# Attention probabilities split into float16 parts and transposed by DMA, V products in float16, second layer in plain float32

## The chip, the cores and the metric

The kernel runs on one core of one Trainium2 chip. The metric is device time in microseconds (us) of one execution. Before the change it is 1511.71 us, the median of 3 runs (1510.98 to 1515.28).

## The reference

Attention keeps only the keys whose score lies within tau of the row's maximum. Its output goes through two layers with a rational function between them.

```python
# q, k, v: (8, 8, 576, 64) float32; tau = 0.02
def _attn_ref(q, k, v, tau):
    scale = 1.0 / np.sqrt(q.shape[-1])
    scores = scale * np.matmul(q, k.transpose(0, 1, 3, 2))
    thresh = np.max(scores, axis=-1, keepdims=True) - tau
    scores = np.where(scores >= thresh, scores, -1000000000.0)
    scores = scores - np.max(scores, axis=-1, keepdims=True)
    attn = np.exp(scores)
    attn = attn / (np.sum(attn, axis=-1, keepdims=True) + 1e-09)
    return np.matmul(attn, v).astype(np.float32)

# x: (4608, 512), the heads side by side; w_in: (512, 2048), w_out: (2048, 512), random doubles
def _moe_ref(x, w_in, w_out, a, b):
    h = x @ w_in
    h2 = h * h
    h3 = h2 * h
    P = a[0] + a[1] * h + a[2] * h2 + a[3] * h3
    Q = 1.0 + np.abs(b[0]) * np.abs(h) + np.abs(b[1]) * h2
    g = P / (Q + 1e-06)
    return (g @ w_out).astype(np.float32)
```

## The kernel before

**Tiles.** There are 8 batches of 4 head pairs. A pair has five units: four full ones of 128 queries of both heads, and a remainder unit that holds the last 64 queries of both heads. That makes 160 units, 128 full and 32 remainders. In the code a unit is named by its pair (0 to 31) and its number in it, so `e13_1` is the probability tile of pair 13, unit 1.

**A unit.** PE multiplies queries and keys in float32 into PSUM (L617, L628). DVE takes the row maximum (L638). Then the mask: in three units of five ACT computes the exponential (L649) and DVE multiplies it with the mask and sums the row (L663); in the other two ACT does both with two activations (L655, L659), a steep leaky ramp and an exponential with a row sum. `BY_ACT` says which. DVE makes the reciprocal of the sum. PE transposes the probabilities in blocks of 128 x 128 float32 (L689, L698 or L701), and with them a tile that repeats the reciprocals (L702). ACT copies the transposed blocks out of PSUM (L263, L706). PE multiplies V with them, with V's 64 columns as weights, one head in each half of the array (L718). DVE multiplies the result by the transposed reciprocals (L723) and two operations split it into a float16 part and a remainder, `xh` and `xl`.

**The layers.** A step takes 256 tokens through two blocks of 128 of the 2048 hidden columns. There are 144 steps. The first layer has 24 float16 matmuls of 256 columns a step (L829), three products of parts of x and w_in. Then ACT and DVE compute the rational function, with a logarithm and an exponential for 1/Q. Its value is split into a rounded part and a remainder (`gh`, `gl`), and the second layer adds three products in the rounded float32 form per block and half of the tokens, 12 matmuls of 512 columns a step (L892).

**The weights** come as doubles. ACT and DVE take them apart once, at the start.

**Order.** Nothing is in a hand-written order. Every operation is entered with its engine, or a choice of engines with a cost for each (`FLEX`), a due time and the buffers and PSUM banks that it takes and gives back. `Plan.order` then goes through them and writes one order for each engine, which the chip keeps: each engine does its instructions in that order and waits where data is not there yet. DMA issues are operations of SP's queue. `POOLS` is the number of buffers of each kind, `PRICE` how a costly engine weighs against a cheap one, `TPD` (new) the cost that the planner puts on a transpose. Until the planner's time 400, it fills part of PE's planned idle time with matmuls whose result is not used (`f_warm`).

The scores of the first 25 units use one bank pair for each head; later units use the one set of three banks (`B3`) for both heads, so the scores of a unit wait until that set is free.

Of the kernel before, what the change touches and what calls it, by code (L numbers as in the profile page):

```python
# [23 lines left out]
POOLS = {"e": 3, "pT": 2, "st": 4, "sc": 2, "t": 9, "g": 2, "x": 4, "xr": 1, "wo": 16}  # L24

B2, B3, BA, B1 = [(0, 1), (2, 3), (4, 5)], [(0, 1, 2)], [(3,), (4,), (5,), (6,), (7,)], [(7,), (6,), (5,), (4,), (3,)]
# [13 lines left out]
BY_ACT = (5, (1, 3))  # L40
# [3 lines left out]
FLEX = {"f1": {"ACT": 0.66, "DVE": 0.345}, "f6": {"DVE": 0.62}, "s1": {"ACT": 0.65, "DVE": 0.396},  # L44
        "d1": {"ACT": 0.55, "DVE": 0.345}, "d2": {"DVE": 0.62}, "qs": {"ACT": 0.7, "DVE": 0.42},
        "s2": {"DVE": 0.66},
        "vmax": {"ACT": 0.58, "DVE": 0.68}, "thr": {"DVE": 0.155}, "rb": {"DVE": 0.16, "ACT": 0.22},
        "tpo": {"ACT": 0.5}, "xh": {"ACT": 0.211, "DVE": 0.15}, "xl": {"DVE": 0.212}, "r": {"ACT": 0.74, "DVE": 0.345},
        "r2": {"DVE": 0.613}, "gl": {"DVE": 0.613}, "gh": {"ACT": 0.541, "DVE": 0.345}}
# [3 lines left out]
PRICE = {"ACT": 1.0, "DVE": 5.0}  # L53

TOL = {"PE": 0.08, "ACT": 0.129, "DVE": 0.1, "POOL": 0.1, "DMA": 0.0}
# [23 lines left out]
class Plan:  # L79
# [3 lines left out]
    LAT = {"PE": 0.27, "ACT": 0.28, "DVE": 0.22, "POOL": 0.16, "DMA": 2}  # L83
    OWN = {"PE": 0.0, "ACT": 0.15, "DVE": 0.13, "POOL": 0.1, "DMA": 2.0}
# [136 lines left out]
def masked_attention_rational_ffn(  # L221
# [159 lines left out]
    def decode_ops(i, key, load, hold, stay):  # L381
# [26 lines left out]
        def f6():  # L408
            t = box["w"].bitcast(I32)
            if stay:  # L410
                tensor_tensor(box["rw"][:, :, 1], t, box["rw"][:, :, 0], ALU.add)
                box["w"] = box["rw"][:, :, 1].bitcast(F32)
            else:
                tensor_tensor(t, t, box["rw"][:, :, 0], ALU.add)

        l = op("DMA", 1.5, key - 2.0, ld, (), [hold])
# [4 lines left out]
        o6 = op(FLEX["f6"], 0, key, f6, [o5, o2], (), [ht if stay else hold])  # L421
        return o6, box, ht
# [7 lines left out]
    for i in range(NW):  # L430
        pieces = []
        for c in range(NC):
# [3 lines left out]
            def load(n=n, c=c, i=i):  # L436
                rw = wpool.tile([P, 2, WS], F32, name=f"rwi{n}", tag="wo", bufs=NF).rearrange("p a b -> p (a b)")
                rw = words(rw)
                nc.sync.dma_start(rw, win_[c * P:(c + 1) * P, 2 * i * WS:2 * (i + 1) * WS].rearrange("p (n two) -> p n two", two=2))
                return rw  # L440
            key = w_key(i, c)

            o6, box, _ = decode_ops(n, key, load, hold, True)
# [25 lines left out]
    for f in range(NF):  # L469
        hold = Hold("wo", 1)  # L470

        def load(f=f):
            rw = words(wpool.tile([P, 2, WS], F32, name=f"rwo{f}", tag="wo", bufs=NF).rearrange("p a b -> p (a b)"))
            nc.sync.dma_start(rw, wout_[f * P:(f + 1) * P, :].rearrange("p (n two) -> p n two", two=2))
            return rw
        key = w_key(f // NC, NC + f % NC)
        o6, box, ht = decode_ops(NC * NW + f, key, load, hold, False)
        ht.uses = 2
        hw = Hold("wo", -1)

        def d1(f=f, box=box):
            wo[f] = wpool.tile([P, 2, WS], F32, name=f"wo{f}", tag="wo", bufs=NF)
            copy(fr(wo[f][:, 0]), box["w"])

        def d2(f=f, box=box):
            tensor_tensor(fr(wo[f][:, 1]), box["w"], wo[f][:, 0], ALU.subtract)
        o9 = op(FLEX["d1"], 0, key, d1, [o6], [hw], [ht])
        wo_done.append(op(FLEX["d2"], 0, key, d2, [o9], (), [ht]))

# [12 lines left out]
    Vs = [const.tile([P, NT * P + 2 * D], F32, name=f"V{i}") for i in range(NV)]  # L502
# [7 lines left out]
    def load_ops(bp):  # L510
# [6 lines left out]

        def ldq():
            nc.sync.dma_start(QQ[0:D, 0:S], qT[bb, pr, :, 0:S])
            nc.sync.dma_start(QQ[D:P, 0:NT * P], qT[bb, pr, :, S + REM:])  # L520
            nc.sync.dma_start(QQ[D:P, S:], qT[bb, pr, :, S:S + REM])

        def ldk():
            nc.sync.dma_start(KK[0:D, REM:], kT[bb, pr, :, 0:S])
            nc.sync.dma_start(KK[D:P, 0:S], kT[bb, pr, :, S:2 * S])

        lq = op("DMA", 0.9, p - (4.6 if first else 4.0), ldq, before)
        lk = op("DMA", 0.9, p - (4.5 if first else 3.9), ldk, before)
# [3 lines left out]
    def load_v_ops(bp):  # L532
# [4 lines left out]
        def ld():  # L537
            nc.sync.dma_start(
                t[:, 0:NT * P].rearrange("p (c d) -> p c d", c=NT),
                v[bb, 0:NT * P, pr * P:(pr + 1) * P].rearrange("(c p) d -> p c d", p=P))  # L540
            for hh in range(2):
                nc.sync.dma_start(
# [13 lines left out]
        l = op("DMA", 1.0, max(q, -2.0 + 0.1 * pr), ld, [av_done.get(bp - NV)])  # L556
        v_done[bp] = l
        hv = [Hold("t", 1)]
        vm_ops.setdefault(bb, []).append(op(FLEX["vmax"], 0, max(q + 1.0, p - 1.0), mx, [l], hv, hv))
        if pr == NP - 1:  # L560
            isx_done[bb] = scale_ops(p, lambda: vms[bb], 14, isx[:, bb:bb + 1], None, vm_ops[bb], f"x{bb}")
# [17 lines left out]
    def unit_ops(bp, t):  # L579
# [6 lines left out]
        QQ, KK, V = QQs[bp % NQ], KKs[bp % NQ], Vs[bp % NV]  # L586
# [3 lines left out]
        e_hold = Hold("e", 2 * nh + 3)  # L590
        st_hold = Hold("st", 1)
        w = P if full else REM
        nb = 2 * NT if full else NT
# [72 lines left out]
        def f_rec():  # L666
            r = box["st"][:, 6:6 + nh]
            engines[plan.eng].tensor_scalar(r, box["st"][:, 4:4 + nh], 1e-9, isx[:, bb:bb + 1], ALU.add, ALU.mult)
# [5 lines left out]
        def f_rb():  # L674
            r = box["st"][:, 6:6 + nh]
            rb = bass.AP(r.tensor, r.offset, [list(r.ap[0]), [1, nh], [0, P // nh]])
# [385 lines left out]
```

## Time and profile before

| | |
|---|---|
| median of 3 runs | 1511.71 us |
| profiled execution | 1513.04 us, its span 1511.1 us |
| granted PE clock, mean | 0.987 |
| PE busy | 1452.7 us, 96% of the span |
| ACT busy | 1267.0 us, 84% |
| DVE busy | 1236.3 us, 82% |
| DMA | 56.39 MB, mean 37 GB/s |

A group's row in the profile gives line, engine, operation, output and inputs, sizes, the count, then busy us and mean ns of one, then idle time of the engine just before and what ended it. Where an engine's instructions overlap, the sum of the groups is above the engine's busy time. A plain float32 matmul of the code appears as two instructions in the trace. Attention is over near 1345 us; what follows are steps of the layers alone.

### The profile page before, as it was taken

Reading aid. Unit: us, or ns where it says so; the run is one execution under the profiler, and the core shown is the slowest. Engines: PE = TensorE matmul, PEld = TensorE weight load, DVE = VectorE, ACT = ScalarE, POOL = GpSimd, SP = SyncE. Lnnn points to the kernel's source line nnn. Section 1 sums busy time; section 2 is a strip of 40 time slices with the busy share of each in tenths; the row PEclk is TensorE's granted clock in tenths of the full one; section 3 lists DMA queues with packets and bytes.
Section 4 is the critical chain, followed back from the end, with each engine's and each line's share of the span. In section 5 each row is a group of like instructions: output and inputs, shape, how many; then the busy total and the mean of one; then the engine's idle time right before and its main releaser. Section 6 shows DMA issues by size and latency. Waiting matters only on the chain.

```text
span 1511.1 us, 29010 instructions
## 1 busy us (share of the span) xinstructions
PE 1452.7 (96%) x11230; PEld 1112.4 (74%) x11230; DVE 1236.3 (82%) x2794; ACT 1267.0 (84%) x2560; POOL 2.3 (0%) x17
## 2 busy tenths in 40 slices
PE   7999896999999999999999999999999999999996
PEld 5676674777777777777777777777777777778774
DVE  7988978979788787869697878787969878877778
ACT  7898987989788898979797979897978798877776
POOL 0000000000000000000000000000000000000000
PEclk9999998999999999999999999999999999999998
DMA  5512301011010100010100010101010010000000
GB/s 155 187 38 88 115 25 58 23 38 39 25 38 25 38 25 31 25 36 12 39 17 31 17 38 25 36 19 39 16 32 25 17 31 17 15 1 15 15 15 14
DMA packets 45241, 56.39 MB, mean 37 GB/s; under 512 B 11824, under 2 KB 28208, under 8 KB 45104
## 3 DMA queue, kind: packets, MB, share of 16 engines
q1 hardware_dynamic: 45104, 54.55, 11.8%
q8 instruction: 88, 1.44, 0.4%
q14 instruction: 49, 0.40, 0.1%
HBM read 45.09 MB, written 9.44 MB: 36 GB/s over the span
## 4 chain that ended last, share of the span: by engine, by line
PE 82%; DVE 7%; ACT 6%; DMA 3%; issue 1%; SPq 1%; ACTq 0%; DVEq 0%
PE banks L892 25%; PE banks L829 21%; PE banks L617 11%; PE banks L718 11%; PE banks L689 8%; PE banks L628 4%; DMA rwo<-in_w_out_dram 1%; PE banks L702 1%; DMA QQ<-in_qT_dram 1%; PE banks L698 1%; DVE st L638 1%; DMA rwi<-in_w_in_dram 1%; DVE e L663 1%; ACT pT L263 1%; ACT vj L553 1%
## 5 line engine op out<-in xcount | busy, mean ns | idle before, releaser
L892 PE MATMUL banks<-wo,gm 128*128 128x512 f32 x1536 | 419.5, 411 | 20.2 <-ACT hsm L838 15.7
L829 PE MATMUL banks<-xh,wi 128*128 128x256 f16 x2048 | 376.1, 273 | 2.9 <-ACT pT L263 2.9
L829 PEld LDWEIGHTS <-wi 128*128 128x128 f16 x3456 | 329.5, 98 | 63.3 <-issue 27.6
L892 PEld LDWEIGHTS banks<-wo,gm 128*128 128x128 f32 x1536 | 274.0, 191 | 80.0 <-ACT hsm L838 17.1
L638 DVE TENSOR_REDUCE st<-banks 128x1 f32<-128x576 f32 x288 | 215.0, 753 | 89.3 <-PE banks L628 53.9
L829 PE MATMUL banks<-xl,wi 128*128 128x256 f16 x1024 | 279.5, 273 | 0.0
L617 PE MATMUL banks<-KK,QQ 64*128 64x512 f32 (+3 forms) x784 | 214.8, 538 | 4.1 <-ACT QQ L271 2.1
L263 ACT COPY pT<-banks 128x512 f32<-128x512 f32 x288 | 164.9, 585 | 51.6 <-PE banks L689 49.9
L718 PE MATMUL banks<-pT,V 128*64 128x128 f32 (+1 forms) x3200 | 195.8, 269 | 5.3 <-ACT pT L706 5.3
L718 PEld LDWEIGHTS banks<-pT,V 128*64 128x64 f32 x3200 | 160.2, 138 | 44.9 <-issue 18.6
L689 PE MATMUL banks<-ident,e 128*128 128x128 f32 x1152 | 166.9, 276 | 9.3 <-DVE e L663 4.8
L689 PEld LDWEIGHTS banks<-ident,e 128*128 128x128 f32 x1152 | 133.4, 145 | 25.0 <-ACT pT L263 4.2
L663 DVE SCALAR_TENSOR_TENSOR e<-banks,st,e 128x576 f32<-128x576 f32 x160 | 126.8, 814 | 19.9 <-ACT e L649 19.4
L617 PEld LDWEIGHTS banks<-KK,QQ 64*128 64x128 f32 (+1 forms) x784 | 88.1, 188 | 66.2 <-issue 47.7
L649 ACT ACTIVATE e<-banks,st 128x576 f32<-128x576 f32 x160 | 118.9, 746 | 1.9 <-DVE st L638 1.9
L628 PEld LDWEIGHTS banks<-KK,QQ 128*128 128x128 f32 x432 | 56.3, 190 | 81.9 <-issue 81.9
L859 DVE SCALAR_TENSOR_TENSOR qm<-qm,cf,Am 128x512 f32<-128x512 f32 x128 | 95.5, 746 | 25.6 <-ACT qm L846 25.3
L655 ACT ACTIVATE e<-banks,st 128x576 f32<-128x576 f32 x128 | 93.9, 742 | 12.1 <-DVE st L642 11.9
L862 ACT ACTIVATE Am<-qm,cf 128x512 f32<-128x512 f32 x128 | 92.6, 723 | 10.9 <-DVE qm L859 8.8
L659 ACT ACTIVATE e<-e,cf 128x576 f32<-128x576 f32 x128 | 98.2, 775 | 0.0
L877 DVE SCALAR_TENSOR_TENSOR rm<-rm,cf,qm 128x512 f32<-128x512 f32 x128 | 95.7, 748 | 1.0
L868 DVE SCALAR_TENSOR_TENSOR rm<-rm,cf,hsm 128x512 f32<-128x512 f32 x128 | 95.6, 747 | 0.7
(121 smaller groups left out, 2101.9 us busy)
## 6 DMA issues: line engine op xcount, KB each, us to landing
KK<-in_kT_dram SPq DMA_DIRECT2D x64, 144.0 KB, 2.9
rwi<-in_w_in_dram SPq DMA_DIRECT2D x16, 512.0 KB, 5.2
V<-in_v_dram SPq DMA_DIRECT2D x32, 256.0 KB, 3.0
rwo<-in_w_out_dram SPq DMA_DIRECT2D x16, 512.0 KB, 4.6
out_dram<-om SPq DMA_DIRECT2D x32, 256.0 KB, 2.1
QQ<-in_qT_dram SPq DMA_DIRECT2D x32, 144.0 KB, 2.8
QQ<-in_qT_dram SPq DMA_DIRECT2D x32, 128.0 KB, 2.7
V<-in_v_dram SPq DMA_DIRECT2D x64, 16.0 KB, 2.5
```

The costliest lines, as they stand in the source:

```text
L263: nc.scalar.copy(dst, src)
L617: nc.tensor.matmul(dst, QQ[r, c0:c0 + P], KK[r, k0:k1], **kw)
L628: nc.tensor.matmul(dst[hh][1], QQ[:, t * P:(t + 1) * P], KK[:, k0:k1], **one)
L638: nc.vector.tensor_reduce(box["st"][:, hh:hh + 1], box["s"][hh], AX.X, ALU.max, negate=True)
L649: nc.scalar.activation(ev(hh), box["s"][hh], AF.Exp, bias=box["st"][:, hh:hh + 1])
L659: nc.scalar.activation(e, e, AF.Exp, bias=ntau, accum_out=box["st"][:, 4 + hh:5 + hh])
L663: nc.vector.scalar_tensor_tensor(ev(hh), box["s"][hh], st[:, 2 + hh:3 + hh], ev(hh), ALU.is_ge, ALU.mult, accum_out=st[:, 4 + hh:5 + hh])
L689: nc.tensor.transpose(box["b", g][:, j * P:(j + 1) * P], box["e"][:, n * P:(n + 1) * P], ident)
L718: nc.tensor.matmul(po[pp, 0:w], V[:, c * P + hh * D:c * P + (hh + 1) * D], rhs, start=c == 0, stop=c == NT)
L829: nc.tensor.matmul(box["ps"][:, j * CT:(j + 1) * CT], wi_tile(c, 2 * fp + j, hl), x[:, c, :], start=c == 0 and n == 0, stop=c == NC - 1 an ...
L877: nc.vector.scalar_tensor_tensor(box["r"], box["r"], a0, box["q"], ALU.add, ALU.mult)
L892: nc.tensor.matmul(acc[tt], fr(box["g"][:, g, o:o + P]), fr(wo[f][:, w, :]), start=begins and j == 0 and n == 0, stop=ends and j == 1 and ...
```

## The change

- The probabilities are scaled by the reciprocal of the row sum first, and split into a float16 part `hi` and a float16 remainder `lo` (`lo` lies in the space of `e`). SP transposes both with one DMA each (L710); PE's transposes and ACT's copies out of PSUM go.
- V is scaled by a power of two per batch and split into `VH` and `VL`. A V product is three float16 products, `VH hi + VH lo + VL hi`, 30 matmuls a unit. The multiplication by transposed reciprocals goes; a constant factor remains.
- The second layer is one plain float32 product with `w_out` as it is (`wp`). The splits of `w_out` and of the rational function's value go.
- The factors that have one source (absolute value, a3 h + a2, b1 |h| + b0) may go to DVE; q becomes a product of two tiles.
- ACT masks in all units.
- Loads of Q, K (but the first), V and the weights are issued by POOL. SP keeps the transposes and the stores.
- The planner's tables change: buffers, bank sets, prices, and the cost of some operations, that of a full unit's scores among them (1.25 to 1.65), whose code is the same.

```diff
-POOLS = {"e": 3, "pT": 2, "st": 4, "sc": 2, "t": 9, "g": 2, "x": 4, "xr": 1, "wo": 16}
+POOLS = {"e": 3, "hi": 3, "pT": 2, "st": 6, "sc": 2, "t": 9, "x": 4, "xr": 1, "wo": 8}
-BY_ACT = (5, (1, 3))
+BY_ACT = (1, (0,))
+UP = 2.0 ** -14
+TPD = 2.5
-PRICE = {"ACT": 1.0, "DVE": 5.0}
+PRICE = {"ACT": 1.0, "DVE": 2.0}
...
+        queue, eng = (nc.sync, "DMA") if first else (nc.gpsimd, "GD")
...
+    def split_v_ops(bp):
+        bb, pr = divmod(bp, NP)
+        p = max(pos[(bp, 0)] - 2.0, pos[(bb * NP, 0)])
+        t, th = Vs[bp % NV], VHs[bp % NV]
+
+        def vh():
+            times(th, t, sx[:, bb:bb + 1])
+
+        def vl():
+            nc.vector.scalar_tensor_tensor(t.bitcast(F16)[:, 0:VW], t, sx[:, bb:bb + 1], th, ALU.mult, ALU.subtract)
+        o = op(FLEX["vh"], 0, p, vh, [isx_done[bb]])
+        v_done[bp] = op(FLEX["vl"], 0, p + 0.1, vl, [o])
...
+        def f_hi(hh):
+            if hh == 0:
+                box["hi"] = sb.tile([P, 2 * S], F16, name=f"hi{name}", tag="hi", bufs=POOLS["hi"])
+                box["lo"] = box["e"].bitcast(F16)[:, 0:2 * S]
+            times(box["hi"][:, hh * S:(hh + 1) * S], ev(hh), box["st"][:, 6 + hh:7 + hh])
+
+        def f_lo(hh):
+            c = slice(hh * S, (hh + 1) * S)
+            nc.vector.scalar_tensor_tensor(box["lo"][:, c], ev(hh), box["st"][:, 6 + hh:7 + hh], box["hi"][:, c],
+                                           ALU.mult, ALU.subtract)
...
+        def f_tp(part):
+            if part == "hi":
+                box["pT"] = sb.tile([P, 2, 2 * NT + 1, P], F16, name=f"pT{name}", tag="pT", bufs=POOLS["pT"])
+            nc.sync.dma_start_transpose(box["pT"][:, part == "lo", 0:nb, :], box[part][:, 0:nb * P])
 
         def f_av():
...
             for c in range(NT + 1):
-                for hh in range(2):
...
-                    nc.tensor.matmul(po[pp, 0:w], V[:, c * P + hh * D:c * P + (hh + 1) * D], rhs, start=c == 0, stop=c == NT)
+                for n, (V, lo) in enumerate(((VH, 0), (VH, 1), (VL, 0))):
+                    for hh in range(2):
...
+                        nc.tensor.matmul(po[pp, 0:w], V[:, c * P + hh * D:c * P + (hh + 1) * D], rhs,
+                                         start=c == 0 and n == 0, stop=c == NT and n == 2)
...
-            qk[0] = qk[1] = op("PE", 1.25, p, lambda: f_qk([0, 1]), need, [sh[0]])
+            qk[0] = qk[1] = op("PE", 1.65, p, lambda: f_qk([0, 1]), need, [sh[0]])
...
+        pt_hold = Hold("pT", 1)
+        tp = op("DMA", TPD if full else 0.6 * TPD, p + 0.6, lambda: f_tp("hi"), his, [pt_hold], [hi_hold])
+        tp = op("DMA", TPD if full else 0.6 * TPD, p + 0.65, lambda: f_tp("lo"), los + [tp], (), [e_hold])
+        bh = bhs["av"] = Hold("b", 2, B1)
+        av = op("PE", 1.0 if full else 0.7, p + 1.2, f_av, [tp, v_done[bp]], [bh], [pt_hold])
...
         def f_q():
-            nc.vector.scalar_tensor_tensor(box["q"], box["q"], b0, box["A"], ALU.add, ALU.mult)
+            nc.vector.tensor_mul(box["q"], box["q"], box["A"])
...
-            for n, (g, w) in enumerate(((0, 0), (0, 1), (1, 0))):
-                nc.tensor.matmul(acc[tt], fr(box["g"][:, g, o:o + P]), fr(wo[f][:, w, :]),
-                                 start=begins and j == 0 and n == 0, stop=ends and j == 1 and n == 2)
+            nc.tensor.matmul(acc[tt], box["r"][:, o:o + P], wo[f], start=begins and j == 0, stop=ends and j == 1)
```

PE around unit 1 of pair 13, before. `e_1_5576` is its probability tile; `KK`, `QQ` are the keys and queries of a later or the same unit.

```order
L617 MATMUL banks<-KK_86,QQ_84 128x512 x2
L628 MATMUL banks<-KK_86,QQ_84 128x64 x2
L689 MATMUL banks<-ident,e_1_5576 128x128 x8
L829 LDWEIGHTS wi
L829 MATMUL banks<-xh_0_3397,wi 128x256
```

The unit's transposes stand behind the scores of a unit and are followed by first-layer matmuls. The same place after the change; `pT_1_6237` is the unit's transposed tile, `wp` the second layer's weights.

```order
L632 MATMUL banks<-KK_86,QQ_84 128x512 x2
L643 MATMUL banks<-KK_86,QQ_84 128x64 x2
L885 MATMUL banks<-wp_109,rm_0_3_6201 128x512 x2
L885 MATMUL banks<-wp_110,rm_0_3_6201 128x512 x2
L824 LDWEIGHTS wi
L824 MATMUL banks<-xh_0_3960,wi 128x256
...
L723 LDWEIGHTS VH_127
L723 MATMUL banks<-pT_1_6237,VH_127 64x128
```

The scores here are those of unit 3. Four second-layer products and six first-layer matmuls stand between them and unit 1's V product, which waits for the two DMAs; no transpose is left on PE. ACT at the same place after the change (`e_1_6178`, `hi_1_6224`: unit 1; `e_2_6245`: unit 2; `Am`, `qm`, `rm`: layer tiles):

```order
L274 ACTIVATE hi_1_6224<-e_1_6178,st_1_6127 128x576
L838 ACTIVATE Am_0_4_6228<-hsm_0_4_6214 128x512
L274 ACTIVATE hi_1_6224<-e_1_6178,st_1_6127 128x576
L845 ACTIVATE qm_0_4_6233<-Am_0_4_6228,cf 128x512
L670 ACTIVATE e_2_6245<-banks,st_2_6217 128x576
L852 ACTIVATE rm_0_4_6254<-hsm_0_4_6214,cf 128x512
L670 ACTIVATE e_2_6245<-banks,st_2_6217 128x576
```

Behind unit 1's second high part stand unit 2's two ramps (L670), whose end frees the bank set for unit 3's scores. SP at the same place, after the change:

```order
L710 DMA_TRANSPOSE pT_0_6180<-hi_0_6134 128x9x128
L710 DMA_TRANSPOSE pT_0_6180<-e_0_6063 128x9x128
L710 DMA_TRANSPOSE pT_1_6237<-hi_1_6224 128x9x128
L710 DMA_TRANSPOSE pT_1_6237<-e_1_6178 128x9x128
L710 DMA_TRANSPOSE pT_2_6324<-hi_2_6311 128x9x128
```

Two transposes a unit stand where loads of Q, K and V stood before; the loads have moved to POOL.

218 lines of the change are left out of this document (88 added, 130 removed).

## The prediction

> **What bounds the kernel now.** The page comes first, then the engines' busy time in four stretches.
>
> ```profile
> PE 1452.7 (96%) x11230; PEld 1112.4 (74%) x11230; DVE 1236.3 (82%) x2794; ACT 1267.0 (84%) x2560; POOL 2.3 (0%) x17
> 0.00:160.00 160.00, 141.68 (x1108) 104.90 (x1109) 135.99 (x394) 138.25 (x306) 2.29 (x17) 0.96 0.38 119
> 160.00:400.00 240.00, 222.87 (x1722) 168.22 (x1721) 203.58 (x466) 204.40 (x412) 0.00 (x0) 0.97 0.15 45
> 400.00:1350.00 950.00, 944.71 (x7491) 722.50 (x7491) 776.02 (x1751) 808.78 (x1636) 0.00 (x0) 1.00 0.09 26
> 1350.00:1511.00 161.00, 143.41 (x916) 116.76 (x914) 120.69 (x185) 115.53 (x209) 0.00 (x0) 0.96 0.04 14
> ```
>
> The columns are stretch, length, then busy time of PE, weight loads, DVE, ACT, POOL, and last the clock, the DMA share and GB/s. From 400 to 1350 us PE is busy 99% of the time, with DVE at 82% and ACT at 85%: PE sets the time there. In the first 160 us PE (89%), DVE (85%) and ACT (86%) are near each other, so a shorter PE does not shorten that stretch by itself. After 1350 us attention is over and only layers run; PE leads again.
>
> Busy PE time includes the tails of pipelined matmuls, so I price PE by the distance between starts, from the chain of waits (first three rows) and the timeline of PE:
>
> ```profile
> 1154.16 2.98 PE banks L892 x12
> 1362.75 7.88 PE banks L829 x72
> 1404.94 5.47 PE banks L892 x24
> 589.26 1.42 PE L617 MATMUL banks<-KK,QQ 128*128 128x512 f32 x6
> 589.70 0.98 PE L617 MATMUL banks<-KK,QQ 128*128 128x512 f32 x5
> 590.51 1.04 PE L689 MATMUL banks<-ident,e 128*128 128x128 f32 x8
> 591.39 0.27 PE L829 MATMUL banks<-xh,wi 128*128 128x256 f16 x1
> 594.33 1.31 PE L718 MATMUL banks<-pT,V 128*64 128x128 f32 x20
> 595.57 1.13 PE L617 MATMUL banks<-KK,QQ 64*128 64x512 f32 x4
> 597.12 0.61 PE L689 MATMUL banks<-ident,e 128*128 128x128 f32 x4
> 603.91 0.80 PE L718 MATMUL banks<-pT,V 128*64 128x64 f32 x20
> 604.65 0.28 PE L829 MATMUL banks<-xh,wi 128*128 128x256 f16 x1
> L617 PE MATMUL banks<-KK,QQ 128*128 128x512 f32 x64 | 32.9, 596 | 0.2 <-ACT pT L263 0.2
> ```
>
> A first-layer matmul costs 7.88/72 = 0.109 us. A second-layer product of 512 columns costs 5.47/24 = 0.228 to 2.98/12 = 0.248, so its three products cost 0.68 to 0.75; I take 0.70. The 589.26 and 589.70 rows are one run, cut once before and once behind its first instruction: a plain float32 instruction of 512 columns takes 0.44. The last row counts 64 of them for the 32 remainder units, whose code has one such product each, so a plain float32 product is two instructions: 0.88. A PE transpose costs (591.39 - 590.51)/8 = 0.11. The V product of a full unit takes 595.57 - 594.33 = 1.24, of a remainder unit 604.65 - 603.91 = 0.74, and the scores of a full unit 597.12 - 595.57 = 1.55.
>
> **PE, in the stretch that it bounds.** Groups of PE from 400 to 1350 us, then the second layer after 1350 us:
>
> ```profile
> L892 PE MATMUL banks<-wo,gm 128*128 128x512 f32 x1060 | 289.6, 408 | 0.5 <-ACT gm L263 0.5
> L718 PE MATMUL banks<-pT,V 128*64 128x128 f32 (+1 forms) x2200 | 133.2, 267 | 1.1 <-ACT pT L706 1.1
> L689 PE MATMUL banks<-ident,e 128*128 128x128 f32 x784 | 112.2, 274 | 0.0
> L702 PE MATMUL banks<-ident,e 128*128 128x128 f32 x110 | 30.0, 273 | 0.0
> L892 PE MATMUL banks<-wo,gr 128*128 128x512 f32 x96 | 26.3, 407 | 0.0
> L892 PE MATMUL banks<-wo,gm 128*128 128x512 f32 x220 | 56.9, 408 | 11.8 <-ACT hsm L838 7.8 <-ACT gm L263 2.5 <-DVE gm L265 0.9
> L892 PE MATMUL banks<-wo,gr 128*128 128x512 f32 x96 | 24.8, 415 | 2.2 <-ACT hsr L838 2.2
> ```
>
> L702 runs once a unit, so 110 units fall here, 88 full and 22 remainders, with 784 + 110 + 110 (L698 or L701) = 1004 transposes.
>
> - Transposes go: 1004 x 0.11 = -110 us.
> - V product: 30 float16 matmuls with 128 streamed columns replace 20 float32 instructions. No row has this form. A float32 instruction with 128 columns costs 1.24/20 = 0.062 and with 64 columns 0.74/20 = 0.037; plain float32 streams each column twice per instruction (0.44 us for 512 columns against 0.109 for 256 in float16), so the 64-column row has the same streaming. I take 30 x 0.037 = 1.10, bounds 0.74 and 1.86: 88 x (1.10 - 1.24) = -12. Remainder units: between half of that rate (0.56) and 1.10, say 0.92: 22 x 0.18 = +4.
> - Second layer: (1060 + 96)/3 = 385 products, each 0.88 in place of 0.70: +69 (bounds +50 and +77).
>
> Sum -49 of 950. PE stays 97% occupied by these prices before (88 x 3.88 + 22 x 2.65 + 96.3 steps x 5.42 = 922 of 950), so I take -46, bounds -30 and -58.
>
> **After 1350 us** there are only layers: (220 + 96)/3 = 105 products x 0.18 = +19. Two operations leave the end of each step (cast and remainder of the activation), which shortens the last chain by about 1.3; 14.0 us of waits ahead of the second layer may hide some of the rest. I take +17, bounds +5 and +20.
>
> **Before 400 us** PE loses about 40 us by the same prices (50 units, 21.5 steps), but it is not alone in front. From 160 to 400 us, where PE is at 93%, its share of this is -13 and I take half, -6; in the first 160 us nothing. Against it, the first V product now waits for four V loads, their scale and the split. Bounds for both together -25 and +20.
>
> **ACT and DVE**, by rows of the groups (shapes apart):
>
> ```profile
> L263 ACT COPY pT<-banks 128x512 f32<-128x512 f32 x288 | 164.9, 585 | 51.6 <-PE banks L689 49.9
> L706 ACT COPY pT<-banks 128x256 f32<-128x256 f32 x160 | 59.9, 375 | 28.8 <-PE banks L702 27.6
> L263 ACT COPY e<-st 128x128 f32<-128x128 f32 x145 | 43.0, 296 | 26.9 <-PE banks L689 21.2 <-DVE qr L874 2.7 <-DVE st L672 2.0
> L263 ACT CAST gm<-rm 128x512 fp32r<-128x512 f32 x122 | 75.4, 618 | 24.3 <-DVE rm L877 18.9 <-PE banks L892 4.7
> L659 ACT ACTIVATE e<-e,cf 128x576 f32<-128x576 f32 x128 | 98.2, 775 | 0.0
> L659 ACT ACTIVATION_READ_ACCUMULATOR e<-e,cf 128x1 f32 x128 | 25.4, 199 | 0.0
> L655 ACT ACTIVATE e<-banks,st 128x576 f32<-128x576 f32 x128 | 93.9, 742 | 12.1 <-DVE st L642 11.9
> L851 ACT ACTIVATE rm<-hsm,cf 128x512 f32<-128x512 f32 x117 | 95.2, 814 | 0.0
> L853 DVE TENSOR_SCALAR rm<-hsm,cf 128x512 f32<-128x512 f32 x11 | 6.0, 544 | 0.0
> L663 DVE SCALAR_TENSOR_TENSOR e<-banks,st,e 128x576 f32<-128x576 f32 x160 | 126.8, 814 | 19.9 <-ACT e L649 19.4
> L278 DVE TENSOR_TENSOR gm<-rm,gm 128x512 fp32r<-128x512 f32 x128 | 87.8, 686 | 5.0 <-ACT gm L263 4.3
> L723 DVE TENSOR_TENSOR pT<-banks,pT 128x128 f32<-128x128 f32 x128 | 36.9, 289 | 23.2 <-PE banks L718 18.0 <-ACT e L655 1.4 <-ACT Am L865 1.1
> ```
>
> ACT loses 164.9 + 59.9 + 43.0 + 75.4 = 343 and about 27 in smaller groups. It gains 160 masking exponentials x (98.2 + 25.4)/128 = 154, 234 high parts between 0.742 and 0.814 (say 0.78) = 183, 27 V casts = 22, and gives DVE 57 of the a3 factors x 0.814 = -46 and some of the absolute values and b1 factors (-34). Net about -90 of row time. DVE loses 127 + 88 + 37 and about 50 in smaller groups. It gains 288 low parts x 0.814 = 234, 54 high parts and 95 linear factors x 0.544 = 81, 32 V low parts x 0.85 = 27, and small copies and absolute values (23); the q product is cheaper by 0.06 each (-9). Net about +55. With 110 of 160 units in the stretch, DVE goes from 776 of 950 to about 814 of 904 (90%), ACT from 809 to about 750 (83%), and PE stays at the top. The scores' bank set comes free after ACT's first mask operation and no longer waits for DVE's mask, which helps PE if anything. I therefore charge nothing for the two engines; without this cover each DVE microsecond per unit would cost 110 us.
>
> **The transposes by DMA.** 256 transfers of 128 x 1152 and 64 of 128 x 640 two-byte elements, alone on SP's queue with the output stores, since the loads move to POOL's.
>
> ```profile
> q1 hardware_dynamic: 45104, 54.55, 11.8%
> V<-in_v_dram SPq DMA_DIRECT2D x32, 256.0 KB, 3.0
> V<-in_v_dram SPq DMA_DIRECT2D x64, 16.0 KB, 2.5
> ```
>
> No row has one. From below: 0.295 MB at the queue's 54.55 MB in 11.8% of 1511.1 us is 0.96 us. From above: the 256 KB load lands in 3.0 us, so 288 KB in 3.4. I take 3.4 for safety. In all they are worth 256 + 64 x 5/9 = 291.6 large ones: 990 us of 1478, no bound. Latency: behind a unit's last high part, ACT's order has a layer operation and two masks with one more between, 4 x about 0.77 = 3.1 us, then PE has the scores of the unit after next (1.55), four second-layer products (3.52) and six first-layer matmuls (0.65) before that unit's V product: 8.8 us of cover for two transfers of 3.4. So they cost nothing, up to 4.4 us each; from 291.6 x T = 1513 on, T = 5.2, their queue is the bound.
>
> The Trainium skill, "DMA: Bandwidth & Descriptors", section "Latency and other measured facts", gives DMA transposes 261 GB/s, by which (an estimate) one takes 1.13 us and all 330 us; that is near the lower row, and the sum would be the same. The Trainium skill, "VectorE: DVE Perf Modes", section "The three transpose paths", speaks against the change: 1309 ns for a 128 x 128 block by DMA and 390 ns on TensorE. Its TensorE figure is not borne out here: blocks leave PE 0.11 us apart. By its DMA figure taken block by block (an estimate) a large transfer takes 11.8 us and all take 3435 us. No row of this trace decides that.
>
> The loads on POOL's queue are due some 4 units (35 us) ahead of use; the quoted landing is 3.0 us, so I put them at nothing.
>
> **Sum.** -46 + 17 - 6 = -35 against the profiled execution's own 1513.0 us (span 1511.1): 1478.0. That execution lies 1.3 above the median 1511.7, so 1477.
>
> **Rivals.**
> 1. *PE's waits shrink no further and no more: all of PE's saving counts.* PE saves 49 + 40 - 19 = 70 in the whole; if DVE and ACT keep up before 400 us too, 1442 (1425 to 1457). For: PE led from 160 us on. Against: DVE gets more work there.
> 2. *DVE becomes the bound.* The low parts and linear factors stand in one queue with the row maxima that free the scores' only bank set; the 35 us are eaten: 1500 to 1522. For: 90% by the sum. Against: 82% today with hardly a PE wait on it.
> 3. *Slower, by PE waiting on that queue.* Each unit's V product waits for a low part queued behind layer work. From 35/160 = 0.22 us a unit the gain is gone; at 0.5 it is 1477 + 80 = 1557 (1522 to 1570).
> 4. *Slower, transposes bound the kernel.* V's load moves 512 packets of 512 B in 3.0 us; if a transpose moves its 295 KB in 1152 pieces of 256 B at that pace, 6.75 us each, 291.6 x 6.75 = 1968 us. It decides from T = 4.4. If blocks of 32 KB are paid one by one, near the 2.5 us of the 16 KB row, nine of them make 22 us and the kernel over 6000; the second page's rule above is the milder form of this.
>
> **How the numbers follow.** Forecast (1457 to 1500) 0.48; rival 1 0.15; rival 2 0.09 (0.03 faster, 0.04 same, 0.02 slower); rival 3 0.16; rival 4 0.12, of which block by block 0.02. About 0.3%, 4.5 us, is what a measurement can tell here. Faster 0.48 + 0.15 + 0.03 = 0.66, same 0.04, slower 0.30. From 1430 to 1550 lie the forecast, most of rival 1, rival 2 and two thirds of rival 3: 0.80.
>
> **What the next profile would show.** Right: no L689 group; second-layer float32 instructions 0.44 apart; V products of about 1.1 us; transposes landing under 3.4 us; PE still near 97% in the middle with DVE near 90%. Wrong: PE waits ahead of the V product released by DMA (rival 4) or by DVE's low parts (rival 3), a V product near 1.9 us, or a middle stretch where DVE is above PE (rival 2).

## The result and the profile after

The changed kernel takes 1500.41 us (median of 5 runs, 1494.62 to 1501.61) against 1511.71 for the kernel before; the ratio is 0.9907 with a 95% interval of 0.988 to 0.9933. It is faster, by 11 us by the medians and 14 by the ratio, where the forecast was 35; the profiled execution has a span of 1498.6 us. Below, a ratio is always against the kernel before on the same chip, and a difference "against the changed kernel" is the difference of two ratios times 1511.7 us, each with some 6 us of interval.

The page of the changed kernel, first its engines, then two rows of the 40 slices and the two large DMA queues (packets, MB, share of 16 engines):

```profile
PE 1411.7 (94%) x11138; PEld 887.2 (59%) x11138; DVE 1261.4 (84%) x2663; ACT 1196.7 (80%) x2248; POOL 161.7 (11%) x300
...
PE   7588769999999999998999999999999999999999
...
PEclk9687879999999999999999999999999999999999
...
q1 hardware_dynamic: 352192, 96.06, 37.3%
q0 software_dynamic: 16160, 44.52, 11.5%
```

The four stretches of the prediction, changed kernel, same columns as there:

```profile
0.00:160.00 160.00, 123.62 (x936) 94.30 (x936) 94.82 (x240) 106.12 (x216) 38.22 (x80) 0.82 0.70 142
160.00:400.00 240.00, 211.91 (x1806) 139.62 (x1807) 211.49 (x468) 205.45 (x386) 32.44 (x59) 0.94 0.61 123
400.00:1350.00 950.00, 931.28 (x7670) 565.43 (x7669) 851.56 (x1794) 797.04 (x1493) 91.01 (x162) 0.99 0.50 93
1350.00:1498.00 148.00, 144.90 (x729) 87.81 (x727) 103.58 (x163) 88.11 (x154) 0.00 (x0) 1.00 0.05 15
```

From 400 to 1350 us the forecast picture holds: PE 98%, DVE 90%, ACT 84%. In the first 160 us all three have become idler: PE 124 us instead of 142, DVE 95 instead of 136, ACT 106 instead of 138, at a clock of 0.82 instead of 0.96. With all three engines idler, something else is waited for.

Counting the V product's instructions up to a time gives the units done by then (20 instructions a unit before, 30 after), the second layer's its steps (12 before, 8 after):

| kernel | units at 60 us | at 100 | at 160 | at 400 | second-layer steps at 400 |
|---|---|---|---|---|---|
| before | 7.0 | 15.2 | 24.0 | 50.0 | 21.5 |
| changed | 1.1 | 6.0 | 15.0 | 43.0 | 17.0 |

At 400 us the changed kernel is 7.0 units, 4.0 first-layer steps and 4.5 second-layer steps behind. By the prediction's prices of before (3.63 a mean unit, 2.62 and 2.80 for the two halves of a step) that is 25 + 10 + 13 = 48 us of PE work. In the changed kernel no layer step runs before 160 us.

Where much of the deficit arises is seen in the timelines of the changed kernel, first PE's:

```profile
48.01 0.25 PE L723 MATMUL banks<-pT,VH 128*64 128x128 f16 x2
62.51 0.32 PE L723 MATMUL banks<-pT,VH 128*64 128x128 f16 x2 [14.26 <-DMA pT<-e]
...
64.14 2.39 PE L632 MATMUL banks<-KK,QQ 64*128 64x512 f32 x4
```

SP's, two transposes in one row, whose issue alone took 15.51 us:

```profile
44.35 15.51 SPq L710 DMA_TRANSPOSE pT<-e  x2
```

And the loads that POOL issues at that time:

```profile
40.89 0.57 POOL L442 DMA_DIRECT2D rwi<-in_w_in_dram  x1
41.72 1.58 POOL L442 DMA_DIRECT2D rwi<-in_w_in_dram  x3 [0.27 <-DVE e L698]
44.32 0.70 POOL L442 DMA_DIRECT2D rwi<-in_w_in_dram  x1 [1.01 <-ACT e L670]
48.25 0.53 POOL L442 DMA_DIRECT2D rwi<-in_w_in_dram  x1 [3.24 <-DVE st L657]
```

Six weight loads of 512 KB start between 41 and 48 us, and the second unit's V product breaks off behind two instructions and waits 14.26 us for a low part's transpose. The first scores after it take 2.39 us for four instructions that take 1.13 in the middle of the kernel; the granted clock from 60 to 80 us was 0.53.

DMA issues of the first 260 us in the changed kernel (KB each, median us from issue to landing):

```profile
rwi<-in_w_in_dram POOLq DMA_DIRECT2D x16, 512.0 KB, 7.9
...
pT<-hi SPq DMA_TRANSPOSE x28, 3.9
pT<-e SPq DMA_TRANSPOSE x28, 4.5
```

The line of the transposes there, shortest, median and longest landing:

```profile
DMA to landing us min/median/max: 2.6/4.3/19.0
```

SP's longest kind of wait in the same time (us in total, times, longest):

```profile
SPq L710 <- PE banks L723: 59.1, 16, 8.0
```

The landing counts from the start of the issue. The two medians add up to 8.4 us for a pair where its two transfers do not overlap, and one alone took up to 19 us. What PE waited for transposes in the same time:

```profile
PE banks L723 <- DMA pT<-e: 26.3, 7, 14.3
PE banks L723 <- DMA pT<-hi: 11.6, 1, 11.6
```

That is 37.9 us. And 16 times SP itself waits to issue one, because both pT buffers are still held by units whose V product has not run. From 400 to 1350 us both parts land in 3.3 us and no engine has a wait for them.

### The profile page after: what moved, and what is told of

It reads as the page before. It is cut to its first block, busy times and chain, and to the rows that moved or that the text cites. A ratio compares the mean times of both kernels' runs of the same rounds, so it can differ in the third digit from the quotient of the medians.

```text
span 1498.6 us, 29343 instructions
## 1 busy us (share of the span) xinstructions
PE 1411.7 (94%) x11138; PEld 887.2 (59%) x11138; DVE 1261.4 (84%) x2663; ACT 1196.7 (80%) x2248; POOL 161.7 (11%) x300
## 3 DMA queue, kind: packets, MB, share of 16 engines
q1 hardware_dynamic: 352192, 96.06, 37.3%
## 5 line engine op out<-in xcount | busy, mean ns | idle before, releaser
L885 PE MATMUL banks<-wp,rm 128*128 128x512 f32 x1024 | 480.8, 604 | 7.7 <-DVE rm L878 7.5
L885 PEld LDWEIGHTS banks<-wp,rm 128*128 128x128 f32 x1024 | 180.9, 191 | 172.7 <-issue 155.1
L670 ACT ACTIVATE e<-banks,st 128x576 f32<-128x576 f32 x288 | 206.5, 734 | 79.4 <-issue 33.8
L698 DVE SCALAR_TENSOR_TENSOR e<-e,st,hi 128x576 f16<-128x576 f32 x288 | 233.2, 810 | 6.8 <-ACT hi L274 6.2
L674 ACT ACTIVATE e<-e,cf 128x576 f32<-128x576 f32 x288 | 220.4, 772 | 0.3
L274 ACT ACTIVATE hi<-e,st 128x576 f16<-128x576 f32 x234 | 177.5, 768 | 29.3 <-issue 18.6
L723 PE MATMUL banks<-pT,VH 128*64 128x128 f16 (+1 forms) x3200 | 151.1, 221 | 38.9 <-DMA pT<-e 26.3
L723 PEld LDWEIGHTS <-VH 128*64 128x64 f16 x3200 | 125.3, 113 | 99.7 <-issue 83.5
L723 PE MATMUL banks<-pT,V 128*64 128x128 f16 (+1 forms) x1600 | 138.1, 219 | 0.0
L723 PEld LDWEIGHTS <-V 128*64 128x64 f16 x1600 | 92.1, 113 | 0.0
L872 DVE SCALAR_TENSOR_TENSOR qm<-qm,Am 128x512 f32<-128x512 f32 x128 | 87.2, 682 | 5.6 <-ACT Am L866 5.3
```

What stands on the lines that cost most here:

```text
L274: nc.scalar.activation(dst, src, AF.Identity, scale=factor)
L670: nc.scalar.activation(ev(hh), box["s"][hh], AF.Prelu, bias=box["st"][:, 2 + hh:3 + hh], alpha=STEEP)
L674: nc.scalar.activation(e, e, AF.Exp, bias=ntau, accum_out=box["st"][:, 4 + hh:5 + hh])
L698: nc.vector.scalar_tensor_tensor(box["lo"][:, c], ev(hh), box["st"][:, 6 + hh:7 + hh], box["hi"][:, c], ALU.mult, ALU.subtract)
L723: nc.tensor.matmul(po[pp, 0:w], V[:, c * P + hh * D:c * P + (hh + 1) * D], rhs, start=c == 0 and n == 0, stop=c == NT and n == 2)
L885: nc.tensor.matmul(acc[tt], box["r"][:, o:o + P], wo[f], start=begins and j == 0, stop=ends and j == 1)
```

## Experiments

Three theories of the lost time at the start: **R**, the round trip of the transfers through few buffers (B in the first four expectations); **C**, contention of the transposes with the weight loads; **S**, the first V product waiting for the scale of four V loads. All runs, with the units counted as above:

| run | median us | ratio (95%) | against the changed kernel | units at 60 / 160 / 400 us |
|---|---|---|---|---|
| more e and pT buffers | 1491.11 | 0.9833 (0.9797 to 0.9869) | -11 | 1.1 / 17.0 / 45.0 |
| plain copies for transposes | 1458.88 | 0.9616 (0.958 to 0.9653) | -44 | 3.0 / 18.9 / 48.0 |
| no bulk of weight loads | 1477.71 | 0.9751 (0.971 to 0.9792) | -24 | 3.0 / 17.0 / 46.0 |
| V scale known | 1491.14 | 0.9834 (0.9799 to 0.987) | -11 | 1.1 / 15.0 / 44.0 |
| copies in the first 25 units | 1457.88 | 0.9623 (0.9581 to 0.9666) | -43 | 3.0 / 19.0 / 48.4 |
| before, second layer plain | 1571.85 | 1.0346 (1.0304 to 1.0388) | | |
| masks undone | 1526.77 | 1.006 (1.0039 to 1.0081) | +23 | |
| buffers, weights later | 1494.9 | 0.9859 (0.982 to 0.9897) | -7 | |
| first 25 units transposed on PE | 1479.61 | 0.9763 (0.9736 to 0.9791) | -22 | 3.0 / 20.0 / 47.0 |
| no bulk and more buffers | 1470.51 | 0.9708 (0.9678 to 0.9739) | -30 | 3.0 / 20.0 / 47.0 |
| more warm products | 1500.74 | 0.9905 (0.9874 to 0.9936) | 0 | 1.1 / 15.0 / 43.0 |

The runs with copies bring rows that are not transposed, the two without the bulk of loads work with one weight tile repeated, and the one with the V scale known scales the first batch otherwise; these five tell of time alone. The runs with copies, and the first one without the bulk of loads, have the same order of instructions on PE, ACT and DVE as the changed kernel in their traces. In the other runs on the changed kernel the planner makes another order (with more warm products on PE alone), and its luck is in the difference too.

**More buffers.**

```diff
-POOLS = {"e": 3, "hi": 3, "pT": 2, ...
+POOLS = {"e": 4, "hi": 3, "pT": 3, ...
```

> The changed kernel with four e and three pT buffers in place of three and two, ordered anew. Three theories of why the first 160 us were lost. B, buffers: e and pT are now held through the whole of a transfer, and SP waited 59 us for V products before it could issue a transpose in the first 260 us; B expects 18 to 19 units done at 160 us where the changed kernel has 15, and 1475 to 1485 us in all (1500 before the edit). C, contention: the transposes are slowed by the 512 KB weight loads beside them; C expects 1496 to 1504, as neither landing nor loads change. S, start: the first V product waits for the scale of all V; S expects 1496 to 1504 as well, with the first V product still near 40 us.

0.7% less, and 17.0 units at 160 us where R expected 18 to 19; the median is 6 to 16 us above the time that R expected. The waits for buffers fell as R says; SP's waits, first 260 us of this run:

```profile
SPq L710 <- PE banks L723: 22.9, 7, 7.6
```

59.1 us of such waits have become 22.9, yet the kernel gained only 11, and in another order. The buffers are at most a part of it, not the whole.

**Plain copies for transposes, everywhere and in the first 25 units.**

```diff
-            nc.sync.dma_start_transpose(box["pT"][:, part == "lo", 0:nb, :], box[part][:, 0:nb * P])
+            nc.sync.dma_start(box["pT"][:, part == "lo", 0:nb, :], box[part][:, 0:nb * P].rearrange("p (n c) -> p n c", c=P))
```

(in the second run only `if single:`, which holds for units 1 to 25)

> The changed kernel with each DMA transpose replaced by a plain DMA copy of the same tile, the same bytes in rows of 1.3 to 2.3 KB: the order on every engine, the waits and the buffers stay, and the V product reads rows that were not transposed. C (contention, in the form that the transposes' small packets are what suffers): landing near 2.5 us and under 6 at the worst, 1470 to 1480 us. C in the form that anything behind the bulk loads suffers: worst landing still over 10 us, 1490 to 1500. B (buffers): the round trip of a pT buffer is shorter by 1.5 to 2 us of some 9, 1488 to 1492. S (start): 1496 to 1504.

> The changed kernel with plain copies in place of the DMA transposes in the first 25 units only (the rows they bring are not transposed); from unit 26 on the transposes stand. Theory R (round trip): in the first 200 us attention runs alone, a unit can start no faster than half the time for which it holds one of the two pT buffers, and so each microsecond of the pair's landing costs half a microsecond a unit there; the pair lands in 8.4 us (3.9 + 4.5) by transposes and in 5.3 by copies, and the run with copies throughout took 2.9% off. R expects nearly all of that here: 1463 to 1473 us. Theory M: the transposes cost along the whole kernel, since 3.3 against 2.4 us holds for all 320; M expects a sixth of it, 1485 to 1495 us.

Both take as good as the same time, 1459 and 1458 us, below every theory's number. Transfers of the first run in the first 260 us:

```profile
pT<-hi SPq DMA_DIRECT2D x26, 288.0 KB, 2.4
pT<-e SPq DMA_DIRECT2D x26, 288.0 KB, 2.9
```

The second run's copies there:

```profile
pT<-hi SPq DMA_DIRECT2D x20, 288.0 KB, 2.4
pT<-e SPq DMA_DIRECT2D x20, 288.0 KB, 3.2
```

The sum of a pair's two landings, 8.4 us, becomes 5.3 to 5.6. PE's waits for transfers all but vanish; the second run, first 260 us:

```profile
PE banks L726 <- DMA pT<-e: 3.2, 2, 1.9
```

That the rest of the kernel keeps its transposes in the second run and loses nothing by it (0.9623 against 0.9616) settles the place: **against plain copies the transposes of the first 25 units cost 43 us, those of the 135 units behind them nothing that can be measured.** The worst form of C (anything behind the bulk loads suffers alike) falls by the time, though its sign came: one copy of the first run took 11.0 us to land, but PE's longest wait for a transfer there was 2.6 us. And SP waits for buffers no less than in the changed kernel; the first run, first 260 us:

```profile
SPq L710 <- PE banks L723: 69.8, 25, 9.7
```

So the 59.1 us of such waits are no measure of what the buffers cost. What these runs don't win back is a late start: their first V product begins at 39 to 40 us, as in the changed kernel, and before at 26 us. By 400 us the second run has caught up but for 1.6 units. Why the first V product comes so late was not taken apart.

**No bulk of weight loads.**

```diff
-                nc.gpsimd.dma_start(rw, win_[c * P:(c + 1) * P, ...
+                if n == 0:
+                    nc.gpsimd.dma_start(w0, win_[0:P, 0:2 * WS]...
+                nc.gpsimd.tensor_copy(rw, w0)
...
-            nc.gpsimd.dma_start(rw, wout_[f * P:(f + 1) * P, :]...
+            nc.gpsimd.tensor_copy(rw, w0)
```

> The changed kernel without 31 of the 32 weight loads: one 512 KB tile is loaded, and POOL copies it into each weight buffer where the load stood, so the weights are one tile repeated and 16 MB of loads are gone. C: transposes land in 3.3 us from the start, worst under 6 us, the waits of PE, ACT and DVE for transposes (26, 19 and 45 us in the first 260 us) all but vanish, 1470 to 1480 us. B: only the single 14 us stall at 48 us goes or shrinks, 1486 to 1494, with 16 to 17 units at 160 us. S: 1496 to 1504.

24 us come back. Transposes in the first 260 us of this run:

```profile
pT<-hi SPq DMA_TRANSPOSE x31, 3.3
pT<-e SPq DMA_TRANSPOSE x31, 3.4
```

And PE's waits for them there, 37.9 us in the changed kernel:

```profile
PE banks L727 <- DMA pT<-e: 5.1, 5, 3.5
```

Without the loads beside them they land as fast as in the middle of the kernel (at worst 9.4 us), in the same order of instructions, so it is the loads that slow them: C holds for 24 of the 43 us. Whether loads issued by SP, as before, would do the same was not tried. The same run with four e and three pT buffers asks whether R and C add:

> The changed kernel without 31 of 32 weight loads (POOL copies one tile, as in the third run) and with four e and three pT buffers. If the early loss is the sum of two things, loads beside the transposes (24 us in the third run) and the buffers' round trip (11 us in the first), they add: 1462 to 1470 us. If both remedies cure the same stalls, no more than the larger: 1475 to 1482 us.

30 us, with 11 + 24 = 35 for a full sum and 24 for none: it lies midway, and the intervals do not allow to call it. In the order that the planner makes with these buffers, taking away the loads is worth 19 us (0.9708 against 0.9833), in the order of the changed kernel 24; the buffers and the order that comes with them are worth 11 us with the loads and 6 without. In the changed kernel's own order the loads are 24 of the 43; the other 19 went only with the shorter transfers, and were not taken apart further.

**V scale known.**

```diff
-        o = op(FLEX["vh"], 0, p, vh, [isx_done[bb]])
+        o = op(FLEX["vh"], 0, p if bb else p - 2.0, vh, [isx_done[bb]] if bb else [v_load[bp]])
```

> The changed kernel with the split of the first batch's V by a constant power of two (the value that the scale has), so that it waits for its own V load alone; maximum and scale are still computed for the layers. S: the first V product moves from 40 us to 30 to 34 us and the time falls to 1490 to 1494. B and C: the pair of transposes that the first V product needs is issued at 31 and 33 us for other reasons (the high parts), so 1497 to 1503.

The maximum of a V can be taken behind its split here, so the first batch's layers are scaled otherwise. The time, 1491, is the one that S expected, but S's sign did not come: the first V product begins at 41.0 us, against 40.0 before this edit, and there are 1.1 units at 60 us and 15.0 at 160 in both. The 11 us were won after that, with 1.0 unit, 1.5 first-layer and 0.9 second-layer steps more at 400 us; the edit orders the later work anew, and why that is better stays open. So another order may be worth as much as the larger buffers.

**More warm products, and weights later.**

```diff
-WARM, WARM_END = 0.6, 400.0
+WARM, WARM_END = 0.9, 400.0
```

> The changed kernel with half as many again of the products of the identity that fill TensorE's planned idle time in the first 400 us (0.9 of it in place of 0.6). Theory K: part of the early loss is the granted clock, 0.82 in the first 160 us against 0.96 before the change, where the scores of a unit take 2.4 us in place of 1.3; K expects the clock to rise to 0.9 and 1485 to 1492 us. Theories R and C: the clock follows from the idle time, and TensorE is not what is waited for there; 1497 to 1505 us.

The stretch from 120 to 160 us in the changed kernel:

```profile
120.00:160.00 40.00, 33.39 (x291) 26.76 (x290) 21.14 (x56) 24.93 (x51) 6.78 (x13) 0.83 0.70 111
```

And with more warm products:

```profile
120.00:160.00 40.00, 35.69 (x381) 28.99 (x380) 22.76 (x63) 27.08 (x57) 8.83 (x16) 1.00 0.81 129
```

The clock rises from 0.83 to 1.00 there, and from 80 to 120 us too, and yet there are 15.0 units at 160 us and 43.0 at 400 in both kernels, and the time is the same. Over the whole first 160 us it rises only from 0.82 to 0.85, since it is lower before 40 us, so the test is fair for 80 to 160 us alone: there the lower clock is not what the time is lost by.

```diff
+POOLS = {"e": 4, "hi": 3, "pT": 3, ...
-WHEN = [(-3.82, 1.63), ...
+WHEN = [(-1.0, 1.63), ...
```

> The changed kernel with four e and three pT buffers, as in the first run, and the first weights' loads and decoding due some three units later. R: the buffers alone gave 0.7%; with fewer weight loads beside the first transposes a little more, 1480 to 1488 us. C (bulk loads beside the transposes): the worst landing falls under 8 us and the time to 1470 to 1480. If the later weights only push the layers back: 1490 to 1500.

0.9859 against 0.9833 with the buffers alone: no difference that the intervals allow to call. C's sign did not come either: the worst landing in the first 260 us is 25.3 us. Loads that come three units later seem to meet other transposes.

**Before, with the second layer alone in plain float32.**

```diff
-            for n, (g, w) in enumerate(((0, 0), (0, 1), (1, 0))):
-                nc.tensor.matmul(acc[tt], fr(box["g"][:, g, o:o + P]), fr(wo[f][:, w, :]), ...
+            nc.tensor.matmul(acc[tt], box["r"][:, o:o + P], wo[f][:, 0, :], ...
```

> The kernel before with one part of the change alone: the second layer in plain float32 (one product in place of three, no cast and remainder of the activation and none of the weights; the buffers that this frees go to the t pool). The prediction's price is 0.18 us more of PE for each of the 576 products: +104 us if PE bounds all of it, and about +88 to +104 with what ACT and DVE give back early: 1590 to 1615 us. The rival: 150 us less on ACT and DVE pay for half of it in the first 400 us and behind 1350: 1545 to 1575 us.

+52 us by the ratio, half of the prediction's price of 104 and inside the rival's range. The chain of waits gives the price of eight instructions, four products:

```profile
191.54 3.63 PE banks L880 x8
```

The stretch from 400 to 1350 us shows who has room:

```profile
400.00:1350.00 950.00, 948.18 (x6680) 616.28 (x6680) 686.51 (x1591) 719.97 (x1415) 0.00 (x0) 1.00 0.09 25
```

3.63/4 = 0.91 us a product, close to the price of 0.88, against 0.70 before. From 400 to 1350 us this kernel does 103 units where before does 110, and some 6 steps fewer: 7 x 3.63 + 6 x 5.42 = 58 us, against the main stretch's +69. Before 400 us it is hardly behind (50 units both, and half a second-layer step less). Behind 1350 us:

```profile
1350.00:1571.00 221.00, 217.23 (x1245) 136.16 (x1244) 148.96 (x255) 148.77 (x278) 0.00 (x0) 1.00 0.04 13
```

PE is busy 98% there, where before it was 89%: the dearer products fill time in which PE waited.

**Masks undone.**

```diff
-BY_ACT = (1, (0,))
+BY_ACT = (5, (1, 3))
```

> The changed kernel with the masks divided as before (two units in five on ACT, the rest on DVE). DVE's 1261 us grow by about 0.6 x 288 x 0.81 = 140 to 1400, ACT's 1197 shrink by about the same. Theory D (DVE is next in the queue): the stretch from 400 to 1350 us is then bound by DVE, 1530 to 1570 us. Theory A (all masks on ACT make ACT the slowest engine in the first 160 us): the early loss shrinks, and the time is 1480 to 1500 us.

23 us slower than the changed kernel: D, at less than its price. The stretch from 400 to 1350 us of this run:

```profile
400.00:1350.00 950.00, 915.91 (x7416) 550.73 (x7416) 889.38 (x1924) 725.99 (x1281) 90.33 (x162) 0.99 0.49 90
```

PE's two longest kinds of wait in it:

```profile
PE banks L885 <- DVE rm L878: 14.1, 12, 4.7
PE banks L824 <- ACT hsm L833: 10.6, 11, 1.4
```

DVE at 94% makes PE wait for the layers' last operation. A's sign is there too, 17.0 units at 160 us in place of 15.0, but two units do not pay for it. Moving the masks to ACT is what keeps DVE at 90%.

**The first 25 units transposed on PE.**

```diff
+        if single:
+            dgs = ...  # ident x reciprocal, one a head
+            for g in range(-(-nb // 4)):
+                ... nc.tensor.matmul(pb[:, o:o + P], box["e"][:, c * P:(c + 1) * P], box["dg", int(c > NT)], ...
+                ... copy(high part, bank)      # ACT or DVE
+                ... tensor_tensor(low part, bank, high part, subtract)
+POOLS = {"e": 4, "hi": 3, "pT": 3, ...
```

> The changed kernel with the first 25 units transposed on TensorE, as products of e with a diagonal of the reciprocals, into PSUM, where ACT takes the high part and DVE the low one (10 small products a unit in place of two transfers), four e and three pT buffers; from unit 26 on the transposes by DMA stand. R (the round trip of the first transfers cost the 43 us): nearly all comes back, as no transfer is waited for and TensorE has idle time there; ACT and DVE get about 0.5 us a unit more, some 12 us: 1462 to 1478 us where the changed kernel has 1500. If ACT and DVE bound the first 160 us by themselves: 1485 to 1500.

2.4% faster than the kernel before and the fastest of the runs that compute the whole result. It has the larger buffers too; against the run that has these alone it is 11 us faster (0.9763 against 0.9833, and the intervals do not meet). Its first stretch:

```profile
0.00:160.00 160.00, 137.76 (x1266) 104.56 (x1266) 118.49 (x335) 125.58 (x277) 40.68 (x85) 0.91 0.31 93
```

The greater part of the new products in the groups of PE, first 200 us (96 half-width ones of L729 add 11.0 us):

```profile
L732 PE MATMUL banks<-dr,e 128*128 128x128 f32 x360 | 58.4, 305 | 6.0 <-DVE pT L740 5.9
```

The products fill time in which PE was idle or ran warm products, whose busy time in the first 160 us is 18 us here and 54 in the changed kernel. At 160 us 20.0 units are done; 22 us come back, half of the 43. The other half is not transfers, for these units have none: ACT's and DVE's extra work and three small stages a unit in place of two transfers may be in it, and so may the order; they were not taken apart.

## Why the prediction was wrong

**The step that failed: "before 400 us", -6, through "so they cost nothing".** The cover of 8.8 us for a pair of transposes was read from an order in which four second-layer products and six first-layer matmuls stand between a unit's high part and its V product. In the first 160 us no layer step runs, so that cover is absent exactly there, and the "before 400 us" term took only the V scale into account, whose removal did not bring the first V product forward. Measured: 43 us for the transposes of the first 25 units, against copies, outside the bound of +20. Two further readings were missing. The weight loads were priced by their own landing, not by what they do to a transfer beside them: 24 of the 43 us. And a pT buffer that was filled by copies from PSUM is now held through two transfers; one more of them, and of e, came with 6 to 11 us, the order's part in which is open. From 400 us on the cover held, with nobody waiting.

**The landing.** 3.4 us was right for the middle (3.3 measured) and wrong for the start (3.9 and 4.5, at worst 19.0). The estimate of 1.13 us a transfer, made from the Trainium skill's throughput in "DMA: Bandwidth & Descriptors" ("Latency and other measured facts"), is not borne out as a landing by the median of 3.3, of which SP's issue alone is 1.2 to 1.4; the throughput itself was not measured here. Nor is the 1309 ns a block of the Trainium skill's "VectorE: DVE Perf Modes" ("The three transpose paths") borne out if it is paid block by block, by which nine blocks take 11.8 us. The sum would have failed by either. The prediction's remark on blocks that leave PE 0.11 us apart compared unlike things: that is a distance between starts, and one transpose on PE lasts 274 ns in the profile.

**The main stretch, -46, was right in sum.** In its 950 us the changed kernel does 7 units, 7 first-layer steps and 5 second-layer steps more than before; by the prices of before 25 + 18 + 15 = 58 us on 922, so before's work takes 950 x 922/980 = 894 us: -56, near the end of the bound (-58). With the copies in the first 25 units it is -51 by the same working. Two errors stand against each other in it. The changed kernel's timeline of PE has the start of a full unit's V product and of what follows (first two rows), of a remainder unit's V product, of two second-layer instructions behind it and of what follows them, and of eight second-layer instructions and what follows:

```profile
701.16 0.30 PE L723 MATMUL banks<-pT,VH 128*64 128x128 f16 x4
...
702.12 1.13 PE L632 MATMUL banks<-KK,QQ 64*128 64x512 f32 x4
...
716.98 0.25 PE L723 MATMUL banks<-pT,VH 128*64 128x64 f16 x4
...
717.57 1.12 PE L885 MATMUL banks<-wp,rr 128*128 128x512 f32 x2
718.63 1.13 PE L632 MATMUL banks<-KK,QQ 64*128 64x512 f32 x4
...
725.88 3.60 PE L885 MATMUL banks<-wp,rr 128*128 128x512 f32 x8
729.41 1.13 PE L632 MATMUL banks<-KK,QQ 64*128 64x512 f32 x4
```

A V product takes 0.96 for a full unit and 0.59 for a remainder, not 1.10 and 0.92: 88 x 0.28 + 22 x 0.15 = -28 where -8 was put. A product of the second layer takes 3.53/4 = 0.88 in a run of eight instructions, as priced, and 1.06 in this one place where two stand alone between other work. By these prices the sum is -110 - 28 + 69 = -69. The 13 us to the -56 are waits of PE, which the prediction put at nothing: all its waits in this stretch add up to 18.4 us, and to 5.1 before. The longest two kinds after the change:

```profile
PE banks L824 <- ACT hsm L833: 9.1, 9, 2.1
PE banks L885 <- DVE rm L878: 4.0, 4, 2.1
```

**After 1350 us, +17 was not lost.** By the prices of before, the kernel before had 25.0 x 2.62 + 26.3 x 2.80 = 139 us of PE work left there and took 161.1 us; the changed kernel had 21.9 x 2.62 + 25.5 x 2.80 = 129 and took 148.6 (its span of 1498.6 less 1350). Both take about 1.16 us for one of this work, so the term is nothing. The price was right, but the waits of before took up all of it: there PE was busy 143.4 of 161 us and waited 14.0 us ahead of the second layer; after the change it is busy 144.9 of 148 without a wait, and its work with 0.88 a product, 21.9 x 2.62 + 25.5 x 3.52 = 147, is nearly the whole stretch. The plain second layer alone showed the same.

**The sum.** -56 + 0 + 47 (the 48 us of deficit at the new pace, 950/980) gives -9, where 11 to 14 were measured. The three parts count the same work, so they show where the time went and not why. The -35 had the main stretch right in sum, gave back 17 that were not lost, and missed some 50 at the start.

**DVE, ACT and the rivals.** 90% and 84% in the middle were right (90% and 83% forecast). Rivals 1, 2 and 4 did not come: not all of PE's saving counted, no engine took PE's place in the middle, and transfers there do not go block by block. That 1500.4 lies where the forecast's range ends and rival 2's begins is chance, for DVE was not what bound the kernel. Rival 3's mechanism, a V product that waits, did come, but behind the transfer and not behind DVE's low part, and only in the first 260 us.

## What to carry to other kernels

A latency that is hidden must be hidden at every place where it occurs: read the cover in the stage that has least of it, most often the start, where the work that should stand between is not there yet. When a step becomes a transfer, the buffers on both its sides are held for its landing, and the bulk loads of that stage are beside it: price the transfer in that company. A mixed form can be better than either, here PE transposes while PE has idle time and DMA transposes once it is full. And where a planner makes the order anew for each run, compare runs of one order: here an edit whose own effect did not show came with 11 us.

## What the runs showed of the hardware

- A DMA transpose of 128 x 1152 two-byte elements lands in 3.3 us against 2.4 for a plain copy of the same bytes, takes SP 1.2 to 1.4 us to issue (a copy 0.46 to 0.57), and moves in small packets: the queue has 352192 packets for 96 MB, stores included. Beside six loads of 512 KB that POOL issued two issues took 15.51 us; beside six more, issued from 204 to 211 us, one transpose took 19.0 us to land.
- The same loads land later too: 7.9 us for 512 KB beside the transposes in the changed kernel's first 260 us, 7.1 beside plain copies, 5.2 in the run that transposes the first 25 units on PE.
- A float16 product with 64 columns of weights and 128 streamed columns costs PE 0.96/30 = 0.032 us, half of the float32 instruction of the same shape (1.24/20 = 0.062).
- Filling idle PE time with products raised the granted clock from 0.83 to 1.00 between 120 and 160 us and brought nothing: 15.0 units at 160 us and the same time.
